# Chunks 2 and 3 of x arrive in columns from DRAM and are normalised there, in place of transposes on TensorE

## The chip, the cores and the metric

The kernel runs on one core of one Trainium2 chip. A time is the device time of one execution in microseconds (us); where several runs are given, it is their median. The profiled execution is a run of its own, recorded with every instruction of every engine: TensorE (PE, and PEld for its weight loads), VectorE (DVE), ScalarE (ACT), GpSimd (POOL) and SyncE (SP). Transfers between DRAM and SBUF are issued on SP and POOL.

## The reference

x has 2048 tokens of 448 features in fp32, the hidden width F is 1792. Cut to what matters:

```python
m = mean(x, axis=-1); v = var(x, axis=-1)
xn = (x - m) / sqrt(v + 1e-5)                       # layernorm, no scale or shift

a = xn @ dft_hid_re.T;  b = xn @ dft_hid_im.T       # DFT along the features
s = dft_seq_re @ a - dft_seq_im @ b                 # real part of the DFT along the tokens

g = silu((gelu(xn @ w_gate) * (xn @ w_up)) @ w_down)
out = x + s * g
```

Every product needs the normalised x. The gate and up products contract over the features, so they want x transposed: features on the partitions, tokens in the columns. The mean and the variance of a token run over the features, that is over a row of x as it lies in DRAM.

## The kernel before, in words

**Split operands.** Every fp32 operand of a product is kept as a high part (an ACT copy into the type `fp32r`, or a DVE copy) and a low part (DVE: source minus high part). A product is three matmuls: high x high, high x low, low x high.

**Chunks.** The 2048 tokens are 4 chunks c = 0..3 of 512. A row of 448 features is padded to 512, so a chunk is four tiles k = 0..3 of 128 tokens by 512 (a partition holds one token), in `xr[c]`. `xr[0]`, `xr[1]` share one buffer (`u0`), `xr[2]`, `xr[3]` another (`u1`). Transposed, a chunk is `xth[c]` and `xtl[c]`, its high and low parts, each with four blocks of 128 features by 512 tokens.

**Layernorm of a chunk (`stats`, L134).** It runs on two or four tiles at a time: `one(i)` makes `bn_stats` and `bn_aggr` on DVE (mean and variance of each token, L140, L141); `root()` takes the square root on ACT (L145) and prepares a factor on DVE; `newton()` is four tiny DVE operations that refine the reciprocal root (L149 to L153); `norm(i)` subtracts the mean and multiplies by the reciprocal root over one 128x512 tile (L158).

**Transposes.** `turn_mm(c, k)` (L164) issues four TensorE transposes of 128x128 of the normalised tile `k` into one of two PSUM banks (kind "tp", banks 4 and 5). `turn_split` (L170) copies the result to `xth` on ACT (L172); for chunks 0 and 1 it makes one more ACT copy of two of the four blocks into `xf` (L175), which the Strassen sums use later; and it subtracts on DVE for `xtl` (L178). After the last tile of a chunk, `whole(c)` (L186) rebuilds the full value in DRAM, in `xw[c]`: SP stores the high parts, POOL adds the low parts with an accumulating transfer. For chunks 0 and 1 it does that for two blocks (512 KB each way), for 2 and 3 for all four (1024 KB each way). Later stages read single blocks back from `xw` (`t_load`).

**Stages.** Each hidden group of 256 is two blocks f. `load_w`, `prep_w`: gate and up weights of f = 0, 1. `gu_mm` (L325) and `first` (L543): gate and up products of one f and one chunk into two PSUM banks of kind "mm" (banks 0 to 3). `act` (L347): GELU on ACT (L351), times the up product on DVE (`m`, L354), high part on ACT (`h`, L355), low part on DVE (`l`). `gateup(f, c, w, between)` (L359) is both, with other work in between. `down_one` (L370): the six matmuls of one tile of 128 tokens with `w_down` (L376) into a bank of kind "o" (banks 6 and 7; kind "po" later), then an ACT copy into `gacc[c]` for the first group (L385), a DVE addition for the later ones (L387). `down` calls it four times for a chunk. `gacc[0]`, `gacc[1]` share a buffer (`a_g[0]`), `gacc[2]`, `gacc[3]` another (`a_g[1]`).

The blocks f = 0 and 1 are done plainly, for all four chunks; this is the part that the change touches. The blocks f = 2 to 13 use a Strassen-like scheme (`strassen`, L412, matmuls L398 and L410) over pairs of chunks; its operands are sums of blocks of the chunks, made on DVE (`sums0`, with `combine`) or from blocks read back from `xw` (`t_load`, `t_step`, `q_steps`). Its weights come with `load_s` on SP (512 KB each) and are summed by `sums_s` and split by `split_s`. After it come the DFT along the features (L989), that along the tokens (L1173 and on) and the output.

**Order.** All is under `manual_schedule` (L505): each engine executes its instructions in the order in which the program issues them, and the two DMA queues take theirs in the order in which SP and POOL reach them. Nothing reorders them; a queued instruction waits until its inputs are there and its output buffer is free. The main part (L506 to L753) is one list written by hand: loads of chunk 0, warm-up matmuls, chunk 0's layernorm and transposes, its gate and up products by halves of 256 tokens, chunk 1's layernorm and transposes in between, statistics of chunk 2 from L613 on and its transposes around `down(0, 0, ...)`, chunk 3's statistics after them. Then a loop over c = 2, 3 (L712) runs gateup(0, c), down(0, c - 1) with chunk 3's transposes as its in-between work, and gateup(1, c). So `down(0, 1)` follows gateup(0, 2).

## Time and profile before

| what | value |
|---|---|
| time, median of 3 runs (lowest to highest) | 774.39 us (774.26 to 774.78) |
| span of the profiled execution | 770.7 us |
| TensorE busy | 764.0 us, 99% |
| VectorE busy | 638.5 us, 83% |
| ScalarE busy | 347.4 us, 45% |
| GpSimd busy | 124.9 us, 16% |
| chain that ended last | PE 95%, DVE 2%, DMA 1% |
| moved by DMA | 165.46 MB, mean 215 GB/s |

The span is the time from the first to the last recorded instruction of one profiled execution; it is shorter than the time of a run by what lies around it. "Busy" sums the time in which an engine executes something. The chain that ended last goes back from the last instruction, at each step to what released it, or to the instruction before it on its engine. In groups of instructions a row has: line, engine, operation, output<-inputs with partitions x elements and type, count | busy us, mean ns of one | idle time of the engine just before them, and what ended most of it. In a DMA row: output<-input, queue, kind, count, KB of each, median us from issue to landing. In lists of single instructions the first number is the start in the span, the second the duration, both in us; "x4" means that four of a kind are taken together. In a table by windows each engine has busy us and the count of instructions in that stretch.

### The profile page before, as it was taken

The numbers are of one execution on the slowest core, as the hardware profiler recorded it, in microseconds if no ns is written. First come the engines' busy times: TensorE is split into PE (matmuls) and PEld (weight loads), VectorE is DVE, ScalarE is ACT, GpSimd is POOL, SyncE is SP. The second block draws the span as 40 slices with busy tenths as digits, with TensorE's granted clock in tenths as the row PEclk, the third lists the DMA queues.
The fourth block names the chain that finished last, engine by engine and source line by source line (L and its number), as shares of the span: only waits on it lengthen the run. The fifth ranks groups of instructions, "written<-read, shape, count | busy, mean of one in ns | idle before, by whom it ended". The sixth has DMA issues, their size and how long they took to land.

```text
span 770.7 us, 11500 instructions
## 1 busy us (share of the span) xinstructions
PE 764.0 (99%) x4052; PEld 688.3 (89%) x4052; DVE 638.5 (83%) x1093; ACT 347.4 (45%) x490; POOL 124.9 (16%) x162
## 2 busy tenths in 40 slices
PE   9999999999999999999999999999999999999997
PEld 8988888888888888888889999999999999999996
DVE  7978989898988988887885676889788796969797
ACT  3756444452533444344334855544444444444441
POOL 2003242332423323323200000000000000000000
PEclk9999999999999999999999999999999999999999
DMA  8479666566767746465652641879797969697894
GB/s 316 91 201 284 153 223 180 148 238 186 252 130 265 199 164 154 154 150 191 138 187 95 268 191 53 255 255 276 262 307 223 343 204 348 189 341 211 311 286 166
DMA packets 81322, 165.46 MB, mean 215 GB/s; under 512 B 8048, under 2 KB 62704, under 8 KB 79728
## 3 DMA queue, kind: packets, MB, share of 16 engines
q1 hardware_dynamic: 75648, 137.15, 51.7%
q0 software_dynamic: 5472, 27.46, 16.7%
q8 instruction: 32, 0.52, 0.3%
q14 instruction: 26, 0.21, 0.1%
q10 hardware_dynamic: 144, 0.11, 0.0%
HBM read 140.71 MB, written 53.35 MB: 252 GB/s over the span
## 4 chain that ended last, share of the span: by engine, by line
PE 95%; DVE 2%; DMA 1%; issue 0%; ACT 0%; SPq 0%; DVEq 0%
PE x L398 24%; PE p L1173 21%; PE po L376 18%; PE p L1176 10%; PE ab L989 9%; PE x L410 4%; PE gu L325 3%; PE py L1193 1%; PE py L1195 1%; PE py L1194 1%; DMA raw<-wgu 1%; PE gu L543 1%; PE pt L167 1%; DVE st L140 0%; DVE xr L158 0%
## 5 line engine op out<-in xcount | busy, mean ns | idle before, releaser
L376 PE MATMUL po<-wd,hs 128*128 128x448 f32 x672 | 152.7, 366 | 0.0
L376 PEld LDWEIGHTS po<-wd,hs 128*128 128x128 f32 x672 | 125.8, 188 | 14.2
L398 PE MATMUL x<-xt,w 128*128 128x512 f32 x450 | 119.4, 391 | 0.0
L398 PEld LDWEIGHTS x<-xt,w 128*128 128x128 f32 x450 | 84.4, 188 | 16.4 <-DVE tmp L444 0.4
L127 ACT ACTIVATE w<-raw 128x896 fp32r<-128x896 f32 (+1 forms) x59 | 53.7, 912 | 63.1 <-DVE raw L1079 35.4
L398 PE MATMUL x<-t,w 128*128 128x512 f32 x276 | 79.7, 391 | 0.0
L387 DVE TENSOR_TENSOR gacc<-gacc,po 128x448 f32<-128x448 f32 x96 | 58.5, 615 | 12.4 <-PE po L376 12.3
L989 PE MATMUL ab<-w,xt 128*128 128x448 f32 x256 | 68.1, 365 | 0.0
L398 PEld LDWEIGHTS x<-t,w 128*128 128x128 f32 x276 | 51.8, 188 | 9.3
L1218 POOL DMA_DIRECT2D cc<-x x14 | 12.4, 882 | 289.3 <-DVE raw L1078 107.8
L475 ACT ACTIVATE hs<-tmp 128x512 fp32r<-128x512 f32 x24 | 15.2, 634 | 97.4 <-DVE tmp L473 97.4
L1173 PE MATMUL p<-xt,w 128*128 128x448 f32 x168 | 54.3, 374 | 0.0
L276 POOL TENSOR_TENSOR raw<-raw 128x256 f32<-128x256 f32 x23 | 18.5, 806 | 211.9 <-DMA raw<-wss 177.4
L989 PEld LDWEIGHTS ab<-w,xt 128*128 128x128 f32 x256 | 48.1, 188 | 3.8
L127 ACT ACTIVATE w<-f 128x896 fp32r<-128x896 f32 (+1 forms) x34 | 30.2, 889 | 42.1 <-DVE f L1079 21.1
L128 DVE TENSOR_TENSOR w<-raw,w 128x896 fp32r<-128x896 f32 (+1 forms) x40 | 41.8, 1046 | 3.3 <-ACT w L127 2.7
L1078 DVE TENSOR_TENSOR raw<-raw 128x128 f32<-128x128 f32 x69 | 19.8, 287 | 21.2 <-DMA raw<-sums 21.1
L293 ACT ACTIVATE w<-raw 128x768 fp32r<-128x768 f32 x24 | 20.3, 846 | 36.7 <-POOL raw L280 36.7
L1173 PE MATMUL p<-ts_u,ts_tmp 128*128 128x448 f32 x112 | 36.3, 374 | 0.0
L1173 PE MATMUL p<-ts_g,w 128*128 128x448 f32 x112 | 36.3, 374 | 0.0
L410 PE MATMUL x<-xt,w 128*128 128x512 f32 x116 | 35.9, 390 | 0.0
L1173 PE MATMUL p<-hs,w 128*128 128x448 f32 x112 | 35.6, 374 | 0.0
(267 smaller groups left out, 1842.8 us busy)
## 6 DMA issues: line engine op xcount, KB each, us to landing
sums<-ca SPq DMA_DIRECT2D x16, 896.0 KB, 8.7
sums<-ca POOLq DMA_DIRECT2D x16, 896.0 KB, 8.6
raw<-ct SPq DMA_DIRECT2D x69, 192.0 KB, 4.4
raw<-wss SPq DMA_DIRECT2D x24, 512.0 KB, 3.9
ts_u<-td SPq DMA_DIRECT2D x24, 448.0 KB, 6.3
ts_g<-td SPq DMA_DIRECT2D x24, 448.0 KB, 6.5
raw<-sums SPq DMA_DIRECT2D x69, 128.0 KB, 4.4
f<-ct SPq DMA_DIRECT2D x39, 192.0 KB, 3.8
```

Source lines behind the costliest of these rows:

```text
L127: nc.scalar.activation(h, src, AF.Copy)
L128: nc.vector.tensor_sub(l, src, h)
L293: nc.scalar.activation(h[:, :n], src[:, :n], AF.Copy)
L325: nc.tensor.matmul(ps[:, cols], a, xt[:, k, cols], start=n == 0, stop=n == len(mm) - 1)
L376: nc.tensor.matmul(po[:, :D], hs[:, a, kk * P : (kk + 1) * P], wdn[:, b, i], start=n == 0, stop=n == 5,)
L387: nc.vector.tensor_add(ga, ga, po[:, :D])
L398: nc.tensor.matmul(ps, a[i], b[j], start=first and n == 0, stop=n == 2, skip_group_check=True)
L410: nc.tensor.matmul(ps, a[0], x_, start=False, stop=True, skip_group_check=True)
L989: nc.tensor.matmul(p[:, :D], a, b, start=n == 0, stop=n == len(mm) - 1)
L1078: nc.vector.tensor_add(s2, cr1, s1)
L1173: nc.tensor.matmul(ps[q][:, :D], h, v, start=u % UN == 0, stop=False, skip_group_check=True)
L1176: nc.tensor.matmul(ps[q][:, :HD], l, v[:, :HD], start=False, stop=u % UN == NS - 1, skip_group_check=True,)
```

## The change

Chunks 2 and 3 get a second input: `xt`, the same values of x in columns, 128 features by (4 blocks x 512 tokens), 1 MB for each chunk, with the four tiles' tokens interleaved (column 4q + k of a block is token q of tile k). The host's array is x itself, permuted. What remains to be done in columns is to subtract a mean and multiply by a reciprocal root that differ from column to column and are the same in every partition.

- `load_xt(2)` brings chunk 2's columns on SP into the buffer of `gacc[2]`, `gacc[3]`, behind the loads of the first weights; `load_xt(3)` brings chunk 3's into `xr[3]`, once its statistics are taken from it.
- Chunk 2's statistics are taken on ACT: four passes `mean2` (negated mean by the sum of a row, `accum_out`) and four passes `square2` (sum of squares around the mean), `root2` on ACT, `newton2` (five operations) on DVE. Chunk 3's stay on DVE (`bn_stats`), in a new order.
- `spread(c)` writes the reciprocal roots and negated means of the 512 tokens to DRAM (`vec[c]`, 4 KB), reads the roots back to all 128 partitions (`tmp(c - 2)`, 256 KB), and adds the negated means to the columns by two accumulating transfers on POOL, each of 512 KB, whose source is one row of 2 KB read by every partition.
- `scale(c, i)` multiplies half a chunk (128x1024) by the roots on DVE; it reads its inputs with a step of four elements and writes the tokens in plain order. `scaled_high` (ACT copy of 128x1024) and `scaled_low` (DVE subtraction of 128x1024) make the two parts. The scaled columns are stored to `xw[c]` by one 1024 KB transfer of SP.
- The transposes of chunks 2 and 3, their `turn_split`, their `norm` and their two accumulating stores are gone.
- `down(0, 1)` now stands ahead of gateup(0, 2), `down(0, 2)` after gateup(0, 3) as before; `down(0, 0)` and `down(0, 1)` take banks 4 to 7 in turn (kind "d") in place of 6 and 7. The loop over c = 2, 3 is written out; `sums_s`, `load_s`, `load_d` and `sums0` have new places in the list.

```diff
-    turns = {"mm": 1, "tp": 0, "o": 0, "x": 0, "po": 0, "all": 0}
+    turns = {"mm": 1, "tp": 0, "o": 0, "x": 0, "po": 0, "all": 0, "d": 3}
...
-        first, n = {"mm": (0, 4), "tp": (4, 2), "o": (6, 2), "x": (0, 5), "po": (5, 3), "all": (0, 8)}[kind]
+        first, n = {"mm": (0, 4), "tp": (4, 2), "d": (4, 4), "o": (6, 2), "x": (0, 5), "po": (5, 3), "all": (0, 8)}[kind]
...
     def whole(c):
-        n = 1024 if c < 2 else 0
-        h, l = [a_x[c][:, 2048 * i + n : 2048 * (i + 1)].bitcast(F32) for i in range(2)]
-        nc.sync.dma_start(xw[c][:, n:], h)
-        nc.gpsimd.dma_start(xw[c][:, n:], l, accum_op=ALU.add)
+        h, l = [a_x[c][:, 2048 * i + 1024 : 2048 * (i + 1)].bitcast(F32) for i in range(2)]
+        nc.sync.dma_start(xw[c][:, 1024:], h)
+        nc.gpsimd.dma_start(xw[c][:, 1024:], l, accum_op=ALU.add)
+    vec = {c: dram.tile([2, 512], F32, name=f"vec{c}") for c in (2, 3)}
+    vt = {c: const.tile([P, 2, 4], F32, name=f"vt{c}") for c in (2, 3)}
+    columns = {2: a_g[1][:, :2048], 3: xr[3].rearrange("p a b -> p (a b)")}
+    scaled = {2: xr[2].rearrange("p a b -> p (a b)"), 3: a_g[1][:, :2048]}
+
+    def load_xt(c):
+        nc.sync.dma_start(columns[c], xt[c - 2])
+
+    def spread(c):
+
+        nc.sync.dma_start(vec[c].rearrange("a (p k) -> p a k", k=4), vt[c])
+        nc.sync.dma_start(tmp(c - 2), vec[c][0].partition_broadcast(P))
+        for i in range(2):
+            nc.gpsimd.dma_start(
+                part(columns[c], 1024 * i, 2, 512),
+                vec[c][1].partition_broadcast(P).unsqueeze(1).to_broadcast([P, 2, 512]),
+                accum_op=ALU.add,
+            )
+
+    def scale(c, i):
+
+        n = slice(1024 * i, 1024 * (i + 1))
+        src = columns[c][:, n].rearrange("p (b q k) -> p b k q", b=2, k=4)
+        dst = scaled[c][:, n].rearrange("p (b k q) -> p b k q", b=2, k=4)
+        r = tmp(c - 2).rearrange("p (q k) -> p k q", k=4)
+        nc.vector.tensor_mul(dst, src, r.unsqueeze(1).to_broadcast([P, 2, 4, P]))
+        if i:
+            nc.sync.dma_start(xw[c], scaled[c])
+
+    def scaled_high(c, i):
+        n = slice(1024 * i, 1024 * (i + 1))
+        nc.scalar.activation(a_x[c][:, n], scaled[c][:, n], AF.Copy)
+
+    def scaled_low(c, i):
+        n = slice(1024 * i, 1024 * (i + 1))
+        nc.vector.tensor_sub(a_x[c][:, 2048:][:, n], scaled[c][:, n], a_x[c][:, n])
...
+        po = in_turn("po" if sends[0] else "d", f"po{gi}_{c}_{kk}")
...
         draw = load_d(GROUPS[0])
+        load_xt(2)
         first(0, half[0], ("hh", "hl", "lh", "last"))
...
+        def mean2(k):
+            nc.scalar.activation(
+                tmp(1)[:, :D], xr[2][:, k, :D], AF.Identity, scale=-1.0 / D,
+                accum_out=vt[2][:, 1, k : k + 1],
+            )
+
+        def square2(k):
+            nc.scalar.activation(
+                tmp(1)[:, :D], xr[2][:, k, :D], AF.Square, bias=vt[2][:, 1, k : k + 1],
+                accum_out=w2[:, 0, k : k + 1],
+            )
+
+        def root2():
+            nc.scalar.activation(w2[:, 1], w2[:, 0], AF.Sqrt, bias=epst, scale=1.0 / D)
+
+        def newton_to(r, t, w):
+            nc.vector.reciprocal(r, t)
+            nc.vector.tensor_mul(t, r, r)
+            nc.vector.tensor_mul(t, t, w)
+            nc.vector.scalar_tensor_tensor(r, t, 1.5, r, op0=ALU.add, op1=ALU.mult)
+
+        def newton2():
+            nc.vector.tensor_scalar(w2[:, 0], w2[:, 0], -0.5 / D, -0.5 * EPS, op0=ALU.mult, op1=ALU.add)
+            newton_to(vt[2][:, 0], w2[:, 1], w2[:, 0])
+
+        mean2(0)
+        mean2(1)
         root()
+        mean2(2)
+        mean2(3)
         newton()
         norm(0)
         norm(1)
         one, root, newton, norm = stats(1, 2, 2)
         one(0)
         one(1)
+        for k in range(4):
+            square2(k)
         root()
+        root2()
         first(0, half[1], ("hh", "lh"))
...
         newton()
         norm(0)
         norm(1)
+        newton2()
+        spread(2)
         turn_split(t0, t1)
-        one, root, newton, norm = stats(2, 0, 4)
...
         one(2)
         one(3)
-        root()
+        load_xt(3)
+        nc.scalar.activation(sd[:, 1], mv[:, :, 1], AF.Sqrt, bias=epst)
+        nc.vector.tensor_scalar(sd[:, 0], mv[:, :, 1], EPS, -0.5, op0=ALU.add, op1=ALU.mult)
+        nc.vector.tensor_scalar(vt[3][:, 1], mv[:, :, 0], -1.0, None, op0=ALU.mult)
         l0()
-        newton()
-        norm(0)
-        norm(1)
+        newton_to(vt[3][:, 0], sd[:, 1], sd[:, 0])
+        spread(3)
         l1()
         first(0, half[1], ("hh", "lh", "hl", "last"), 1, pg)
-        norm(2)
-        norm(3)
         m0, h0, l0 = act(0, 1, pg)
         m0()
         pg = gu_ps(1, 1)
         for g in range(2):
             gu_mm(pg[g], ws[1], g, 1, slice(0, 512))
-        turn_split(turn_mm(2, 0))
         h0()
-        between = [lambda k=k: turn_split(turn_mm(2, k)) for k in (1, 2, 3)]
-        turn = between[0]
-        between[0] = lambda: (turn(), l0())
-        down(0, 0, wdn, between)
+        scale(2, 0)
+        l0()
         m1, h1, l1 = act(1, 1, pg)
-        one, root, newton, norm = stats(3, 0, 4)
-        one(0)
-        one(1)
+        scaled_high(2, 0)
         m1()
         h1()
-        one(2)
-        one(3)
-        root()
-        l1()
-        newton()
-        norm(0)
-        norm(1)
+        scale(2, 1)
+        down(0, 0, wdn, [l1, lambda: scaled_high(2, 1), lambda: scaled_low(2, 0), lambda: scaled_low(2, 1)])
+        draw = load_d(GROUPS[1])
+        load_s(2)
+        down(0, 1, wdn)
         t0 = {}
...
-        for c in (2, 3):
...
-            down(0, c - 1, wdn, between)
...
+        scale(3, 0)
+        scaled_high(3, 0)
+        scale(3, 1)
+        scaled_high(3, 1)
+        scaled_low(3, 0)
+        scaled_low(3, 1)
+        sums_s(nc.vector)
+        m0, h0, l0 = gateup(0, 2, ws[0])
+        m0()
+        h0()
+        l0()
+        sums0()
+        m1, h1, l1 = gateup(1, 2, ws[1])
+        m1()
+        t_load(0, 0, 3, 2)
+        h1()
+        l1()
+        for v in split_s(slots[0]):
+            v()
+        w_of[0, 2] = parts_of(slots[0])
+        load_s(3)
+        m0, h0, l0 = gateup(0, 3, ws[0])
+        m0()
+        h0()
+        l0()
+        down(0, 2, wdn, [lambda: t_split0(1), lambda: t_split0(2)])
+        nwdn, low_d = prep_d(GROUPS[1], draw)
+        m1, h1, l1 = gateup(1, 3, ws[1], [lambda: t_split0(3), lambda: (t_split0(4), q_steps[0][0]())])
+        m1()
         late = (h1, l1)
```

59 lines of the change are left out of this document (16 added, 43 removed).

## The prediction, made before the changed kernel ran

> **What bounds the kernel now.** I read the first part of the page for the whole, then what TensorE waited for, then the chain of waits over the first 140 us, where the change lies. In the groups the columns are busy time, mean ns of one, and idle time before; in the chain they are start, duration, what.
>
> ```profile
> span 770.7 us, 11500 instructions
> PE 764.0 (99%) x4052; PEld 688.3 (89%) x4052; DVE 638.5 (83%) x1093; ACT 347.4 (45%) x490; POOL 124.9 (16%) x162
> PE warm L524 <- DVE hs L514: 1.5, 1, 1.5
> PE gu L543 <- ACT xt L172: 0.3, 1, 0.3
> 20.85 0.19 DVE mv L141
> ...
> 21.07 0.30 ACT sd L145
> 21.37 0.98 ACT xt L172 x2
> ...
> 22.39 1.69 PE gu L543 x12
> 24.08 1.03 PE pt L167 x8
> 25.11 3.84 PE gu L543 x32
> 28.95 5.02 PE gu L325 x22
> 33.97 0.44 PE pt L167 x4
> ...
> 54.34 0.44 PE pt L167 x4
> ...
> 67.18 5.02 PE gu L325 x22
> 72.19 4.08 PE x L398 x18
> ```
>
> TensorE is busy 99%, and its recorded waits are the start-up and 0.3 us at 22.4 us. From 22.39 us on the chain runs through TensorE without a gap, through the first Strassen product at 72.19 us and beyond. So there are two regimes. Before 22.4 us the chain hops between DVE and ACT: a delay there moves everything. After it only TensorE work, or a new wait of TensorE, counts.
>
> **Removed: eight groups of transposes.** Chunks 2 and 3 lose 32 transposes, eight groups of four. The chain has them one by one, the first at 33.97 and the last at 54.34 us, each 0.44 us: 8 x 0.44 = 3.52 us off TensorE's path. Their 8 ACT copies and 8 DVE subtractions, the 8 normalisations and two accumulating 1024 KB transfers into `xw` go too; all lay beside TensorE work, so they are worth nothing directly, but they make room for what is added.
>
> **Added in the head: chunk 2's statistics on ACT, its Newton steps on DVE.** Eight passes over 128x448 (four `mean2`, four `square2`) and a second root enter ACT between 16.0 and 21.1 us; five tiny DVE operations (`newton2`) enter DVE between chunk 1's normalisation and its first `turn_split`.
>
> ```profile
> 7.25 1.28 SPq L132 DMA_DIRECT2D xr<-x  x3
> 2.03 0.20 ACT L518 ACTIVATE tbl<-epst 128x1 f32<-128x1 f32 x1
> 15.37 0.67 ACT L175 ACTIVATE tmp<-pt 128x256 f32<-128x256 f32 x2
> 16.62 0.30 ACT L145 ACTIVATE sd<-mv,epst 128x2 f32<-128x2 f32 x1 [0.59 <-DVE mv L141]
> 22.20 1.00 DVE L158 TENSOR_SCALAR xr<-xr,mv,sd 128x512 f32<-128x512 f32 x2
> 23.12 1.28 DVE L178 TENSOR_TENSOR xt<-pt,xt 128x512 fp32r<-128x512 f32 x2
> 24.45 0.42 PEld L167 LDWEIGHTS pt<-ident,xr 128*128 128x128 f32 x4 [0.17 <-DVE xt L178]
> xr<-x SPq DMA_DIRECT2D x3, 1024.0 KB, 8.2
> L385 ACT ACTIVATE gacc<-po 128x448 f32<-128x448 f32 x12 | 6.5, 543 | 6.2 <-PE po L376 6.2
> L172 ACT ACTIVATE xt<-pt 128x512 fp32r<-128x512 f32 x14 | 8.1, 594 | 5.9 <-PE pt L167 5.9
> L355 ACT ACTIVATE hs<-tmp 128x512 fp32r<-128x512 f32 x8 | 5.0, 633 | 5.1 <-DVE tmp L354 5.1
> L152 DVE TENSOR_TENSOR sd<-sd 128x4 f32<-128x4 f32 x2 | 0.3, 168 | 0.1
> ```
>
> Chunk 2 is the middle one of the three loads issued from 7.25 us, so it is issued near 7.7 and, at the middle landing time of 8.2 us, there by 15.9: no wait for it. A pass reads SBUF: the copy of 128x448 took 0.543, and a copy of 128x512 from SBUF 0.633 where one from PSUM took 0.594, so about 0.58. Each waits for the one before (about 0.03), so 0.61 for a mean. The squares also take their bias from a tile: the root of 128x2 with its bias took 0.30 and the 128x1 one without that second operand 0.20, so 0.71. No row shows what the added sum per row costs. The low end is nothing, the high end one more smallest instruction of 0.30 us each. A copy with 448 elements is the nearest row in every respect but that output, so I take nothing and keep 8 x 0.30 = 2.4 us for the range.
>
> ACT is free at 15.37 + 0.67 = 16.04. Two means end at 17.26, chunk 1's first root (0.30) at 17.56, still before DVE asks for it at 17.8; two means end at 18.78, four squares at 21.62. The second root, which starts at 21.07 before, starts 0.55 later. DVE is late by that, then runs five operations of 0.17 + 0.03 = 1.0 us, and only then the two subtractions (23.12 us before). The next transposes reuse the banks those free: the idle 0.17 us at 24.45 shows TensorE already waiting there, so the delay passes on whole. Head: 0.55 + 1.0 = +1.55 us; the copies at 21.37 slip 0.85 by the second root and lie inside that. A gain is excluded, nothing is removed before 22 us.
>
> **Chunk 2's columns must arrive in time.** The path is `newton2`, a 4 KB write of statistics, then on POOL two accumulating transfers of 512 KB that add the negated mean, read from one 2 KB row by every partition, then `scale`. `scale(2,0)` stands on DVE between the product of gate(0,1) and what that chunk still needs; `scaled_high(2,0)` stands on ACT ahead of h1 and of the eight PSUM drains L385 of the moved down products. If the transfer is late, DVE and ACT stop with all that queued, and TensorE stops at chunk 1's first down product, for which bank 4 and h1, l1 are needed.
>
> ```profile
> 33.18 0.60 ACT L351 ACTIVATE tmp<-gu 128x512 f32<-128x512 f32 x1
> xw<-xt POOLq DMA_DIRECT2D x2, 512.0 KB, 5.8
> xw<-xt POOLq DMA_DIRECT2D x2, 1024.0 KB, 8.0
> cc<-x POOLq DMA_DIRECT2D x14, 224.0 KB, 6.8
> sp<-xt SPq DMA_DIRECT2D x4, 512.0 KB, 10.4
> xr<-x SPq DMA_DIRECT2D x2, 256.0 KB, 2.8
> out<-cc SPq DMA_DIRECT2D x1, 112.0 KB, 1.7
> ```
>
> Need: the GELU of (0,1) at 33.18 ends 33.78; later by 1.55 and one more small DVE operation (0.20) it ends at 35.5, the product at 36.2, where `scale(2,0)` can start; `scale(2,1)` follows a scale, l0 and m1, at 38.5. Supply: `newton2` ends at 23.2 + 0.55 + 1.0 = 24.75; the small write lands 1.7 to 2.8 later, at 26.5 to 27.5; an accumulation of 512 KB took 5.8 (into SBUF, for 224 KB, 6.8), so the first half is there at 32.3 to 34.3; the two halves together are 1024 KB, 8.0, so the second at 34.5 to 35.5. Spare time: 1.9 us or more on the first, 3.0 on the second. I cost it at nothing. TensorE has some 0.7 us in hand (its chunk 0 down products end near 40.3, l1 near 40.9 is wanted a bit later), so a second half later than 38.5 by x costs x - 0.7. The column load itself (1 MB behind the weights on SP at about 9 us) has until 27 us. On POOL the accumulation for `xw1` now stands behind those of chunk 2; its reader comes after 46 us. SP holds `load_d` and `load_s(2)` behind `scale(2,1)`, near 39.7, as they are held until 40.5 us before.
>
> Chunk 3 has its Newton steps at 34.4, its statistics in DRAM by 37.5, so columns by 37.5 + 8.0 = 45.5; TensorE needs them near 55, after 24 + 24 down products (9.7 us) and two gate/up products of 5.02 us each. DVE in between has two scales, two lows, the sums of `load_s(2)`, four sums of chunk 0 and 1 and the products of chunk 2 queued, some 12 us: done by 57.5, wanted at 60. The store of `xw3` leaves at 46.6 the buffer that the down products of chunk 2 fill from 60 us; even at 8.0 us it is gone. Nothing. That `down(0,1)` moves ahead of gateup(0,2) exchanges TensorE work of the same length, and its four banks replace two: nothing either.
>
> **The scales.** Each is a product of 128x1024 whose two inputs are read with a step of 16 bytes; no row shows such a step.
>
> ```profile
> L297 DVE TENSOR_TENSOR w<-raw,w 128x768 fp32r<-128x768 f32 x1 | 1.0, 951 | 0.0
> L315 DVE TENSOR_TENSOR wd<-raw,wd 128x896 fp32r<-128x896 f32 x1 | 1.1, 1074 | 0.0
> L209 DVE TENSOR_TENSOR tmp<-tmp 128x512 f32<-128x512 f32 x1 | 0.7, 684 | 0.0
> L689 DVE TENSOR_TENSOR tmp<-tmp 128x512 f32<-128x512 f32 x1 | 1.2, 1222 | 0.0
> ```
>
> From 768 to 896 elements is 0.123 us, so 1024 take 1.20: the low end. The high end is the slowest that DVE ran such an operation, 1.222 against 0.684 for 512, 1.79 times, so 2.14. Plain rows of this shape are nearest, I take 1.20: then `l1` of (1,1) ends near 40.4 and TensorE does not wait. At 2.14 the two scales ahead of l1 bring it 1.9 us later, of which TensorE has about 0.9 in hand: +1.0 us.
> [...]
>
> **The sum.** -3.52 + 1.55 = -1.97 us. The profiled span of 770.7 us stands 3.7 below the median of 774.39 of the three runs; what lies around the span I take as fixed. 774.39 - 1.97 = 772.4 us. What a measurement of this kernel can tell from no change is about 0.2%, 1.55 us: faster is below 772.8, slower above 775.9.
>
> **Rivals.**
> - *The new instructions are dear.* Row sums at up to 0.30 each (+2.4), strided scales (+1.0). For it: neither output nor step is in any row. Against it: at the low ends it vanishes. With a 0.20 read-out the time is 772.4 + 1.6 = 774.0, with the scales 775.0, with both high ends 775.8: within 0.2%. Chance 0.29.
> - *The spread is late* (the other side). 128 partitions read one 2 KB row, and the transfers accumulate into SBUF. If the halves go one after the other at 6.8 us the second lands at 41 and costs 1.8 us, 774.2; at the 10.4 us that 512 KB took when the queues were full, 27.5 + 20.8 = 48.3, 9.1 us, 781.5. It eats the whole gain when the second half lands later than 38.5 + 0.7 + 1.97 = 41.2, and is slower by over 0.2% from 42.7. For it: no row repeats a source, and the DMA engines are 0.72 and 0.70 busy from 25 to 35 us already (last column but one below). Against it: 3 us to spare, and part of that load (the accumulation for `xw1`) now comes after. A middle case is 777. Chance 0.31, of which 0.27 beyond the bound.
>  [...]
> - *The statistics hide.* If ACT's passes finish before 21.07, only `newton2` is left: 774.39 - 3.52 + 1.0 = 771.9. Chance 0.04.
>
> ```profile
> 25.00:30.00 5.00, 5.00 (x40) 4.78 (x39) 4.82 (x9) 4.71 (x9) 0.09 (x1) 1.00 0.72 193
> 30.00:35.00 5.00, 5.00 (x26) 4.24 (x25) 4.72 (x15) 4.23 (x6) 0.79 (x1) 1.00 0.70 103
> ```
>
> **How the numbers follow.** The forecast has 0.36; its own range is 771.4 to 772.8. With the statistics hidden (0.04) it makes faster 0.40. Dear instructions give 0.24 and a spread late by little 0.04 to same, 0.28. The spread beyond the bound, 0.27, and both high ends with some lateness on top, 0.05, make slower 0.32. The range goes from 771.2 to 779.5 and leaves out a badly late spread.
>
> **What the changed profile would show.** The chain without transposes between 30 and 60 us and the first Strassen product near 70.2 us. TensorE idle near 22 to 26 us some 1.5 us longer; far more would mean that the row sums cost. Scale operations of 1.2 us; 2.1 would mean the step costs. No wait of DVE for a transfer into `gacc` or `xr`; a wait there, with TensorE idle at a down product near 40 us, would make the prediction wrong by just that wait.

## The result: 793.5 us, 2.6% slower

| | before | after |
|---|---|---|
| time, median of the runs taken side by side (4 and 4) | 774.33 us (772.99 to 774.78) | 793.53 us (793.07 to 794.11) |
| span of the profiled execution | 770.7 us | 792.2 us |

The ratio is 1.0256, with a 95% interval of 1.0241 to 1.027. The forecast was 772.4 us with a range up to 779.5, so the kernel is 19 us slower where a gain of 2 was forecast.

The first rows are the head of the page of the kernel after; behind the dots stand the larger waits of TensorE over the whole execution (us in total, times, longest).

```profile
span 792.2 us, 11454 instructions
PE 768.1 (97%) x4020; PEld 683.8 (86%) x4020; DVE 640.3 (81%) x1078; ACT 349.4 (44%) x500; POOL 129.8 (16%) x164
...
PE po L410 <- DVE hs L390: 4.8, 1, 4.8
PE po L410 <- ACT gacc L419: 2.4, 1, 2.4
PE po L410 <- ACT hs L389: 2.0, 1, 2.0
...
PE x L432 <- ACT tmp L490: 1.5, 2, 1.0
PE x L432 <- DVE tmp L483: 1.3, 4, 0.5
PE x L432 <- DVE tmp L511: 1.2, 1, 1.2
PE x L432 <- DVE tmp L522: 1.0, 1, 1.0
```

Before, TensorE had one wait of 0.3 us after its start. After, it waits 9.2 us at three down products (`po`) and some 6 us in the Strassen stage (`x`), a stage that the change does not touch. So there are two losses, and they come at different times. The first Strassen product starts at 82.65 us where it started at 72.03 before: 10.6 us late. The last matmul of the kernel starts 21.9 us late. Half of the loss lies ahead of the first Strassen product and half behind it.

**The early loss.** Next come single instructions of the kernel after, taken from its lists by engine and brought together by subject: the two transfers that add chunk 2's means and the two for chunk 3 (POOL), the four scales (DVE), and what TensorE does at the gate and up product of 30 us, at its waits and at the first Strassen product. The brackets give the idle time in front of an instruction and what ended it.

```profile
28.47 1.23 POOL L202 DMA_DIRECT2D gacc<-vec  x1 [2.26 <-DMA vec<-vt]
38.69 1.22 POOL L202 DMA_DIRECT2D gacc<-vec  x1 [8.99 <-issue]
46.57 1.23 POOL L202 DMA_DIRECT2D xr<-vec  x1 [5.72 <-issue]
54.30 1.21 POOL L202 DMA_DIRECT2D xr<-vec  x1 [6.50 <-issue]
...
38.46 2.01 DVE L214 TENSOR_TENSOR xr<-gacc,tmp 128x1024 f32<-128x1024 f32 x1 [2.31 <-DMA gacc<-vec]
46.27 1.97 DVE L214 TENSOR_TENSOR xr<-gacc,tmp 128x1024 f32<-128x1024 f32 x1 [4.61 <-DMA gacc<-vec]
54.01 2.02 DVE L214 TENSOR_TENSOR gacc<-xr,tmp 128x1024 f32<-128x1024 f32 x1 [2.89 <-DMA xr<-vec]
60.94 1.97 DVE L214 TENSOR_TENSOR gacc<-xr,tmp 128x1024 f32<-128x1024 f32 x1 [4.92 <-DMA xr<-vec]
...
30.36 5.18 PE L359 MATMUL gu<-xt,w 128*128 128x512 f32 x22
42.81 1.29 PE L410 MATMUL po<-wd,hs 128*128 128x448 f32 x5 [2.41 <-ACT gacc L419]
48.90 5.58 PE L410 MATMUL po<-wd,hs 128*128 128x448 f32 x19 [4.79 <-DVE hs L390]
82.65 0.84 PE L432 MATMUL x<-xt,w 128*128 128x512 f32 x3
```

Against them stand these rows of the kernel before: the same gate and up product, one group of the transposes that are gone and the product behind it, and the first Strassen product.

```profile
28.78 5.18 PE L325 MATMUL gu<-xt,w 128*128 128x512 f32 x22
33.80 0.60 PE L167 MATMUL pt<-ident,xr 128*128 128x128 f32 x4
34.16 1.47 PE L376 MATMUL po<-wd,hs 128*128 128x448 f32 x6
72.03 0.84 PE L398 MATMUL x<-xt,w 128*128 128x512 f32 x3
```

Every scale waits for its transfer. Chunk 2's halves are there at 38.4 and 46.2 us, where the forecast had 34.3 and 35.5 at the latest, and chunk 3's second half at 60.9 instead of 45.5. The second transfer of a pair is issued only when the first has landed: POOL stands idle for 9 us in front of it, and no instruction of the program is named as the reason ("issue"). Behind the waiting scale stand the low parts of chunk 1 on DVE and the drains of the down products on ACT, and TensorE stops for both, as the prediction had said of a late transfer.

The stops cost a second time. These are the busy times of the engines and TensorE's granted clock (column behind POOL) in three stretches of the kernel after:

```profile
40.00:45.00 5.00, 1.70 (x7) 0.88 (x6) 1.67 (x3) 2.55 (x4) 0.85 (x1) 1.00 0.81 101
45.00:50.00 5.00, 1.10 (x3) 1.01 (x4) 3.73 (x4) 1.72 (x3) 1.23 (x1) 0.53 1.06 192
50.00:55.00 5.00, 5.00 (x21) 4.47 (x20) 2.11 (x2) 2.21 (x5) 0.70 (x1) 0.79 1.02 314
```

TensorE's clock is at one half from 45.3 to 52.1 us, 6.8 us long; the first stop lies at 40.40 to 42.81 us, the second at 44.11 to 48.90. In 48.9 to 52.1 it works at that clock, and a matmul starts each 0.37 us there and each 0.20 behind it, which costs 1.6 us. The account up to the first Strassen product reads: +1.6 that the head is late (28.78 to 30.36), -2.9 for the transposes (a group takes 0.36 us from its start to the start of the next product, 33.80 to 34.16), +9.2 of waits, +1.6 of clock, together +9.5 of the 10.6 us. The remaining 1.1 us are about what the matmuls at the edges of the stops lose: by their starts, the one ahead of a stop takes some 0.16 us more than others, the one behind it 0.10.

**The late loss.** In the Strassen stage each block loads its weights (`raw<-wss`) on SP, and POOL sums them. In the fence are SP's issues and POOL's work near 134 us, in the kernel after. Behind the second dots stands the row of the DMA queue that fetches instructions, counted between 133.5 and 135.5 us alone (packets, MB, share of the 16 DMA engines).

```profile
133.52 0.33 SPq L294 DMA_DIRECT2D raw<-wss  x1
133.96 1.88 SPq L295 DMA_DIRECT2D raw<-wss  x1
...
140.02 0.74 POOL L310 TENSOR_TENSOR raw<-raw 128x256 f32<-128x256 f32 x1 [10.94 <-DVE tmp L470]
144.54 1.65 POOL L840 DMA_DIRECT2D sums<-ca  x2
147.30 0.33 SPq L294 DMA_DIRECT2D raw<-wss  x1
...
q8 instruction: 1, 0.02, 4.6%
```

The same load in the kernel before, POOL's accumulating transfers behind it, and the next load:

```profile
120.28 0.39 SPq L261 DMA_DIRECT2D raw<-wss  x1
128.06 1.68 POOL L775 DMA_DIRECT2D sums<-ca  x2
133.62 0.33 SPq L260 DMA_DIRECT2D raw<-wss  x1
```

The second issue takes 1.88 us, where the same issue of the kernel before takes 0.39, and a 16 KB transfer of that instruction queue runs at the same moment. The load lands at 139.86 (5.9 us after its issue; before 3.7), and POOL's sums begin 0.16 us behind that; the row names a DVE instruction as what ended the wait, and I take the load for it, which the row of the restored kernel below names. The accumulating transfers `sums<-ca`, which stand on POOL behind the sums, are issued at 144.54. They come 2.8 us ahead of the next load of weights, where before it was 5.6. That load then takes 10.0 us (before 7.2), and TensorE waits for what hangs on it. Two more fetches fall on loads of weights in this stage: the issue `raw<-wd` at 222.56 us takes 2.27 us, where others take 0.38, and that at 252.32 us takes 0.38 beside a fetch at 252.26. From 75 to 330 us no fetch falls on an issue of SP in the kernel before. The experiments below test whether the fetch is the cause.

### The profile page after: what moved, and what is told of

Read it like the earlier page. It is cut to its first block, busy times and chain, and to the rows that moved or that the text cites. A ratio compares the mean times of both kernels' runs of the same rounds, so it can differ in the third digit from the quotient of the medians.

```text
span 792.2 us, 11454 instructions
## 1 busy us (share of the span) xinstructions
PE 768.1 (97%) x4020; PEld 683.8 (86%) x4020; DVE 640.3 (81%) x1078; ACT 349.4 (44%) x500; POOL 129.8 (16%) x164
## 4 chain that ended last, share of the span: by engine, by line
PE 66%; DVE 13%; DMA 11%; ACT 4%; issue 3%; POOL 1%; SPq 0%; DVEq 0%; POOLq 0%; ACTq 0%
PE p L1238 18%; PE x L432 13%; PE po L410 10%; PE ab L1054 9%; PE p L1241 9%; DMA raw<-wss 3%; PE x L444 3%; DMA tmp<-xw 2%; DMA ts_g<-td 2%; PE py L1258 1%; PE py L1260 1%; PE py L1259 1%; DMA tmp<-vec 1%; DMA vec<-vt 1%; DVE w L324 1%
## 6 DMA issues: line engine op xcount, KB each, us to landing
sums<-ca POOLq DMA_DIRECT2D x16, 896.0 KB, 10.2
```

## The experiments

A time "at the first Strassen product" is the start of TensorE's first `x` matmul after the start of the span. It stands against 72.03 us in the kernel before. "Late at the end" is the time by which the last matmul is late.

### Without the mean subtraction

The kernel after without its four accumulating transfers: columns, statistics, roots, scales and order stay. Its output lacks the subtraction of the mean in chunks 2 and 3.

```diff
-        for i in range(2):
-            nc.gpsimd.dma_start(part(columns[c], 1024 * i, 2, 512),
-                vec[c][1].partition_broadcast(P)..., accum_op=ALU.add)
```

> The changed kernel without the two pairs of accumulating transfers that add the negated means: the columns are scaled as they came, so the output lacks the means; everything else, the statistics included, stays. Theory A (the late second accumulation is the cause): scale(2,0) finds its input ready at 36.2 us, the chain has no DMA into gacc or xr, TensorE has no gap over 1.5 us between 35 and 55 us, and of the 21.8 us that TensorE ends later only the head (+1.4 us at 30 us) and about 1.2 us for the dear scales remain against the 3.52 us of transposes: 774.4 - 3.5 + 1.4 + 1.2 = 773.5 us, 772 to 776. Rival B (the order of the work, DVE's scales and lows ahead of the sums and the products, is too much whatever DMA does): over 783 us. Rival C (half and half, other transfers of the change are late too): 776 to 783 us.

Measured: 778.4 us, ratio 1.0063 (1.0046 to 1.0081), above theory A's 776 and in the range of rival C. Rival C's reason is not what the trace shows: TensorE has no recorded wait from 28 to 75 us, and the first scale starts at 36.34 us, where the prediction needed it at 36.2. The first Strassen product starts at 70.94 us, 1.1 earlier than before. So the four transfers make all of the early loss: with them 10.6 us late, without them 1.1 us early. Of the 2.0 us that the sum promised for the early stage, 1.1 are there once the transfers are gone: in this execution the head costs 1.8 us, and the missing transposes gain 2.9. Yet the run is slower than the kernel before: from -1.1 it goes to +5.6 us at 257 us and to +6.6 at the end. The late loss is there without a late transfer.

A second run leaves out, beside the means, the interleaved order of the columns, so that the scales read and write plain rows.

> As the run without the means, and the scales read and write their 128x1024 elements in plain order, so that the tokens come out permuted: the same count of elements with no step of 16 bytes. Theory A: the scales take 1.2 us in place of 1.99 us, and TensorE's small waits at chunk 1's down products go: 772.3 us, about 1.2 us under the run without the means. Rival: the step costs more than that, because the four scales stand ahead of later work on DVE: 4 x 0.8 = 3.2 us under it. If the scales still take 2 us, the cost is not the step but the broadcast operand.

Measured: 778.2 us, ratio 1.0051 (1.0034 to 1.0068). The row has two scales of this run; with the step they took 1.97 to 2.02 us, as shown above:

```profile
L207 DVE TENSOR_TENSOR xr<-gacc,tmp 128x1024 f32<-128x1024 f32 x2 | 2.4, 1219 | 0.0
```

A step of 16 bytes costs 0.8 us per scale: 2.0 against 1.22. The forecast's choice of 1.20 fits the plain rows and was wrong for the step. The time shows no effect of it, against the theory (1.2 us) and the rival (3.2 us): the two runs differ by 0.2 us. This was tested only where the means are not added and the scales have room.

### The head alone

The kernel before with the statistics of chunk 2 on ACT, the second root and `newton2`, which are computed and stored and not used.

> The kernel before, with the eight passes of statistics on ACT, the second root, the five operations on DVE and the small write of 4 KB added at the places that the change gives them; the results are not used, chunks 2 and 3 keep their transposes and their own statistics. Theory A: the head alone costs what the changed trace shows at 30 us, +1.4 us, and it goes through to the end: 775.8 us (775.2 to 776.5). Rival: work that follows has slack for it, 774.4 us, within 0.4. Rival: more than the shift, because DVE is later for all that follows by the same amount: over 777 us.

Measured: 774.95 us, ratio 1.002 (1.0003 to 1.0038); the first Strassen product comes 0.98 us late and the end 0.92. TensorE's matmuls ahead of the head are 0.5 us early in this execution, so the head costs 1.5 us, what the forecast made it. (The +1.4 of the expectations sets the chain's 28.95 us against 30.36; from start to start it is 1.58.) The lateness stays between 0.9 and 1.2 us from there to the end: a delay of 1 us alone brings no late loss.

### Why the columns are late: the row, the queue, or the accumulation

The first kernel writes the row of means twice, so that a partition's 4 KB come as one piece instead of two of 2 KB.

```diff
...
-                part(columns[c], 1024 * i, 2, 512),
-                vec[c][1].partition_broadcast(P).unsqueeze(1).to_broadcast([P, 2, 512]),
+                columns[c][:, 1024 * i : 1024 * (i + 1)],
+                vec[c][1:].rearrange("a d -> (a d)").partition_broadcast(P),
```

> The negated means stand twice in DRAM, so that each accumulating transfer of 512 KB has 128 rows of 4 KB in place of 256 rows of 2 KB; one 2 KB write more on SP, nothing else changed. In the changed kernel the second transfer of a pair was issued 10.2 us after the first, 0.25 us after the first had landed, though POOL was free and no wait of the program stands before it; the accumulation for xw1, of 128 rows, was issued 0.7 us after that second one without waiting. Theory A1 (the queue of POOL holds a limited number of rows, over 384 and under 512): the second is now issued within 2 us of the first, both have landed near 40 us in place of 46.3, and the time falls to about 780 us (774 to 787). Rival (an accumulation into SBUF waits for the one before, whatever its rows): the second still waits for the first, 793 us, within 1.5.

The second lets each partition read its own 4 KB of `xt` instead of the one row.

```diff
-                vec[c][1].partition_broadcast(P).unsqueeze(1).to_broadcast([P, 2, 512]),
+                xt[c - 2][:, 1024 * i : 1024 * (i + 1)].rearrange("p (a d) -> p a d", a=2),
```

> The changed kernel, but the four accumulating transfers read 128 distinct rows of the column array in place of the one row of means for all partitions (so what is added is not the negated mean). Sizes, descriptors and targets are the same. Theory (accumulating 1 MB into SBUF takes about 14 us whatever it reads): the second half of chunk 2 still lands 16 to 19 us after the first was issued, time 790 to 796. Rival (the one row, read 128 times over, is the limit): both halves land within 10 us of the first issue, at 35 to 39 us, DVE does not wait for them, and the time falls to 780 to 786.

Measured: 792.99 us, ratio 1.0244 (1.0227 to 1.0262), for the wide rows; 787.66 us in one run for the own rows. POOL's issues and the second scale of chunk 3 in each, wide rows ahead of the dots:

```profile
29.04 1.78 POOL L203 DMA_DIRECT2D gacc<-vec  x2 [1.60 <-DMA vec<-vt]
60.74 1.96 DVE L215 TENSOR_TENSOR gacc<-xr,tmp 128x1024 f32<-128x1024 f32 x1 [1.31 <-DMA xr<-vec]
```

```profile
25.14 2.15 POOL L202 DMA_DIRECT2D gacc<-xt  x2
56.61 1.96 DVE L214 TENSOR_TENSOR gacc<-xr,tmp 128x1024 f32<-128x1024 f32 x1 [1.85 <-DMA xr<-xt]
```

In pieces of 4 KB both transfers of a pair are issued together ("x2"). So POOL's 9 us of "issue" hang on how a transfer is cut: with 256 pieces of 2 KB the second was issued 10.2 us behind the first (28.47 and 38.69), with 128 of 4 KB both took 1.78 us together. That half of the theory held; the landing near 40 us and the time near 780 did not come. The pair still needs 14.5 us from the first issue to the second landing (29.04 to 43.51, where the kernel after had 46.25), and chunk 3's columns are ready at 60.7 as before: the small write of its means now takes 12.0 us, so its pair is issued at 47.03 us only. The own rows came out as 4 KB pieces too (864 packets on POOL's queue from 24 to 62 us in both, 1376 in the kernel after), so they are compared with the wide rows and not with the kernel after, as their expectation had it. They need 14.05 us (25.14 to 39.19), and the time lies between the ranges of the theory and the rival. One row or 128 rows makes a difference of 0.4 us for a pair, in one execution of each. In the kernel after, half a megabyte from one row landed 7.6 us after its issue (38.69 to 46.25).

The own rows are 5 us faster than the wide ones. They don't wait for the statistics: their first pair is issued 3.9 us earlier and chunk 3's, at 42.58 us, 4.5. They show what the early loss hangs on. The second scale of chunk 3 starts at 60.94, 60.74 and 56.61 us in the kernel after, with wide rows, and with own rows; the first Strassen product follows at 82.65, 83.80 and 78.31 us, 21.7 to 23.1 us later each time.

### Without accumulation at all

Here the means go to all partitions with a plain transfer of 256 KB, POOL adds them in place, both chunks' variances come from `bn_stats`, and the gate and up products of chunks 2 and 3 take the high parts first. This and two later kernels hold 32 or 16 matmuls of 16x16 in the warm-up; the section after next tells why.

```diff
+    def shift(c):
+        for i in range(2):
+            v = part(columns[c], 1024 * i, 2, 512)
+            nc.gpsimd.tensor_add(v, v, tmp(0).unsqueeze(1).to_broadcast([P, 2, 512]))
```

> A version without accumulating transfers: both chunks come in columns, the negated means come by a plain 256 KB transfer that spreads one row over the partitions, and POOL adds them in place; the variances come from bn_stats on DVE at their old places; gate/up of chunks 2 and 3 take the high parts first; with the 32 small matmuls. Theory (the accumulating transfers and nothing else in the column scheme made the change dear in the early stage): first Strassen product at 68.5 to 74 us against 72.0 before, time 771 to 776. Rival (the strided scales and the queues of DVE and ACT make it dear, however the means come): DVE late at gate/up of chunk 2 and 3 by 3 us or more each, 778 or more.

Measured: 784.9 us, ratio 1.013 (1.009 to 1.0169), the first Strassen product 9.0 us late. The rival's time came. Its waits came in part: TensorE waits 2.4 us at the gate and up products of chunk 2 and 1.6 at those of chunk 3, under the 3 us each that it named. A further 2.5 us, at a down product, have a reason that neither had named. Single instructions of that kernel on POOL and DVE:

```profile
31.82 4.70 POOL L204 TENSOR_TENSOR gacc<-gacc,tmp 128x1024 f32<-128x1024 f32 x2 [6.38 <-DMA tmp<-vec]
31.98 2.25 DVE L655 TENSOR_TENSOR sd<-vt 128x4 f32<-128x4 f32 x1
34.26 2.28 DVE L656 TENSOR_TENSOR sd<-sd 128x4 f32<-128x4 f32 x1
...
47.42 0.17 DVE L655 TENSOR_TENSOR sd<-vt 128x4 f32<-128x4 f32 x1
```

A DVE operation on 128x4 takes 0.17 us, and 2.25 and 2.28 while POOL adds 128x1024: the second ends at 36.54 us, POOL's additions at 36.52. The low part that the down product waits for stands on DVE behind these two. While POOL makes chunk 3's two additions, three more DVE operations, two of 128x1024 and one of 128x512, take 7.4 us in place of 3.1. So POOL's additions are not free work. How much of the 9.0 us hangs on them was not tested apart.

### Chunk 3 alone in columns

Chunk 2 stays as it was before. Chunk 3's means are taken early on ACT, and its transfers are issued at 25.6 us, 30 us ahead of their use.

> One part alone: only chunk 3 comes in columns, chunk 2 stays as in the kernel before. Chunk 3's means are taken by ACT early and its accumulating transfers are issued near 20 to 27 us, some 30 us ahead of their use; 16 small matmuls stand for its 16 removed transposes. Theory (the scheme itself is sound where the 14 us of the accumulation lie ahead of their use): no wait of TensorE for the scaled columns, four groups of transposes less (-1.8 us), head +0.3 to +0.6 us for the means: 773 to 774.5. Rival (the strided scales and the fuller queues of DVE and ACT in chunk 2's and 3's stage cost more than the transposes): TensorE waits some 3 us at gate/up of chunk 3, 776 to 778.

Measured: 779.13 us, ratio 1.007 (1.0045 to 1.0095), above both ranges. The accumulation is hidden: it lands at 34.8 us, 9.2 us after its issue. Now the roots are late, which come from `bn_stats` at the old place. The second kernel computes and sends them earlier, ahead of the weight loads on SP.

```diff
-        draw = load_d(GROUPS[1])
-        load_s(2)
         spread_root()
...
+        load_s(2)
+        draw = load_d(GROUPS[1])
```

> Only chunk 3 in columns again, with its roots sent earlier: the statistics of chunk 3 stand on DVE between the splits of chunk 2, the spread of the roots leaves SP ahead of the weight loads instead of behind them, and the sums of the weights stand behind the scales on DVE. Theory (the 4.2 us that TensorE waited in the run before hung on the roots, which landed at 55.5 us): the roots land by 50 to 52 us, TensorE waits 1 us or less at gate/up of chunk 3, first Strassen product at 70.5 to 72.5 us, time 772 to 775. Rival (the scales and the lows, some 8 us of DVE and ACT, are the limit): still 2 us or more of waits, 776 to 779.

Measured: 779.87 us, ratio 1.0064 (1.0047 to 1.0081), above both ranges again. TensorE's waits for the scaled columns fall from 4.2 to 3.0 us and the first Strassen product from 76.75 to 74.42 us. The roots of 256 KB are still late. The first row is chunk 3's scales in the first kernel, the second one in the second:

```profile
55.58 3.86 DVE L222 TENSOR_TENSOR xr<-gacc,tmp 128x1024 f32<-128x1024 f32 x2 [4.78 <-DMA tmp<-vec]
```

```profile
53.90 3.88 DVE L222 TENSOR_TENSOR xr<-gacc,tmp 128x1024 f32<-128x1024 f32 x2 [5.27 <-DMA tmp<-vec]
```

DVE is idle for 5 us in front of the scales in both. The theory (roots by 50 to 52 us) failed: the transfer was issued 3.7 us earlier, at 45.75, and took 8.1 us instead of 6.0, with an accumulation for `xw` and the weight loads beside it. Neither kernel with chunk 3 alone beat the kernel before; chunk 2 alone was not tried.

### The late loss: instruction fetches

The pieces of 16 KB on the queue q8 "instruction" come 32 times in the kernel before (0.52 MB) and 31 times in the kernel after (0.51 MB). I read them as TensorE's instructions, by their number: 4052 matmuls with as many weight loads make 253 for each piece, and the 4020 of the kernel after 259. From the first piece to the last (17.57 to 760.97 us before, 20.04 to 769.50 after) TensorE starts 7876 matmuls and weight loads in 31 intervals before and 7601 in 30 after, 254 and 253 for an interval; the expectations below put it at 256. The change takes 32 transposes, 64 instructions with their weight loads, out of the front of that stream, so each later piece is asked for at another point of the work: at 116.6 us before, between two loads of weights; at 134.0 us after, on a load. To test this, 32 matmuls of 16x16 that compute nothing needed stand in place of four of the warm-up matmuls. They bring the count back.

```diff
-        warm(WARM)
+        warm(WARM - 4)
+        t = o_tile("tiny")
+        for _ in range(32):
+            nc.tensor.matmul(t[:16, :16], junk[:, :16], junk[:, :16], start=True, stop=True)
```

Once in the kernel without means, once in the whole changed kernel:

> The kernel without the mean subtraction (778.4 us), with 32 matmuls of 16x16 put in place of four of the fourteen warm-up matmuls at the start, so that TensorE's stream has again as many instructions ahead of the Strassen products as before the change. Theory (the late loss comes from the fetch of TensorE's instructions, 16 KB every 256 instructions, which falls on the load raw<-wss of the three-block products): the fetch falls at 116 to 118 us again as in the kernel before, the load ahead of 133 us takes about 7.2 us instead of 9 to 10.5, and the stretch from the first Strassen product to the end is as long as in the kernel before within 1 us: 772.5 to 774.0. Rival (the late loss comes from the order in which the queues reach the Strassen stage, whatever is fetched): 778.4 again, within 1 us, with the same waits of TensorE for DVE's tmp at about 135, 178 and 220 us.

> The changed kernel whole, with the same 32 matmuls of 16x16 in place of four warm-up matmuls. Theory of the fetch: the early loss stays (about +10.6 us at the first Strassen product), of the later 11.2 us some 6 go: 786 to 789. Rival (the later loss is a matter of the order of the queues): 793.5 within 1.5.

And the other way round: the kernel before with nothing of the change, its stream shifted by 192 instructions.

```diff
-        warm(WARM)
+        t = o_tile("tiny")
+        for _ in range(96):
+            nc.tensor.matmul(t[:16, :16], junk[:, :16], junk[:, :16], start=True, stop=True)
+        for _ in range(WARM):
+            nc.tensor.matmul(t[:, :288], junk[:, :P], junk[:, :288], start=True, stop=True)
```

> The kernel before with nothing of the change, but with 96 matmuls of 16x16 added to the warm-up, whose 14 matmuls are cut from 512 to 288 columns so that it takes about as long. TensorE's stream is so shifted by 192 instructions, as far against a raster of 256 as the 64 that the change takes away shift it the other way. Theory (the place of the instruction fetches alone makes the late loss): the fetch that fell at 116.6 us falls near 120 or 133 us, one of the loads raw<-wss there takes over 4.5 us, and the stretch from the first Strassen product to the end is 3 to 6 us longer: 777 to 780. Rival (the late loss belongs to the change itself): 774 to 775.5.

In the table, the lateness at 100, 130 and 257 us is that of one matmul, counted from the first Strassen product on, against its time in the kernel before.

| kernel | time | ratio (95%) | late at the first Strassen product | at 100 us | at 130 us | at 257 us | late at the end |
|---|---|---|---|---|---|---|---|
| after | 793.53 | 1.0256 (1.0241 to 1.027) | +10.6 | +13.9 | +13.7 | +20.7 | +21.9 |
| after, count restored | 787.29 | 1.0159 (1.0127 to 1.019) | +11.6 | +14.2 | +13.9 | +14.6 | +14.8 |
| without means | 778.4 | 1.0063 (1.0046 to 1.0081) | -1.1 | +1.0 | +0.8 | +5.6 | +6.6 |
| without means, count restored | 775.22 | 1.0002 (0.9987 to 1.0018) | -0.3 | +1.1 | +0.9 | +1.5 | +3.8 |
| before, count shifted | 782.21 | 1.01 (1.0077 to 1.0124) | +0.5 | +4.5 | +4.6 | +9.1 | +10.2 |

The columns of lateness compare one execution of each kernel with one of the kernel before, whose span of 770.7 us is short: the runs of the kernel before beside these experiments have spans with medians from 772 to 773 us. By the medians of the times the five kernels are 19.2, 12.5, 4.6, 0.4 and 7.2 us slower, 2 to 3.4 less than the last column.

Shifting the stream alone makes the kernel before 1% slower, more than the theory's 777 to 780, with 9.7 of its 10.2 us behind the first Strassen product. Restoring the count takes 8.1 us of the late loss out of the changed kernel (11.3 to 3.2), within the theory's range, and 3.5 out of the one without means (7.6 to 4.1), whose time lies 1.2 us above the theory's range. What it takes out stands between 130 and 257 us: the changed kernel loses 7.0 us there, and 0.7 with the count restored. SP's issues and POOL's at the same load show the path, first in the changed kernel with the count restored, then in the shifted kernel before:

```profile
134.16 0.38 SPq L295 DMA_DIRECT2D raw<-wss  x1
137.95 0.74 POOL L310 TENSOR_TENSOR raw<-raw 128x256 f32<-128x256 f32 x1 [9.74 <-DMA raw<-wss]
141.87 1.65 POOL L843 DMA_DIRECT2D sums<-ca  x2
```

```profile
124.91 1.27 SPq L261 DMA_DIRECT2D raw<-wss  x1
134.17 1.66 POOL L779 DMA_DIRECT2D sums<-ca  x2
```

With the count restored the issue is back at 0.38 us, POOL starts at 137.95 instead of 140.02, and the accumulation leaves 2.7 us earlier. Where the fetch falls on it, the issue takes 1.27 us. From that issue to the accumulation it is 7.8 us in the kernel before, 10.6 in the changed one, 7.7 with the count restored and 9.3 in the shifted one. That the place of the fetch sets most of the late loss is shown from both sides. The step within, that the fetch itself holds up SP's issue, is read from the coincidence in these rows and was not tested apart.

Not all of the late loss goes this way. Between the first Strassen product and 100 us, in the table's terms, DVE waits for one load `tmp<-xw` of 256 KB, on whose issue no fetch falls. It lands 5.0 us after its issue in the kernel before, 10.5 in the changed kernel, 9.5 with the count restored and 13.0 in the shifted kernel. So 2.6 of the 3.2 us that remain with the count restored stand there, and 4.0 of the shifted kernel's 9.7. What makes that load late is open. In the restored kernel without means 2.3 of the remaining 4.1 us come behind 600 us, and their cause is open too. The restored kernels have four warm-up matmuls fewer and reach the first Strassen product 0.8 and 1.0 us later than the same kernels without the small matmuls; the one without means starts its first gate and up product at 10.65 us, the kernel before at 9.09.

### Filling the stops

The clock's fall was tested in the changed kernel: 28 matmuls that compute nothing needed stand where TensorE waits, 10 ahead of the first stop and 18 ahead of the second.

```diff
+                if (gi, c, kk, n) == (0, 1, 0, 5):
+                    fill(18, wdn)
...
+        fill(10, wdn)
         down(0, 1, wdn)
```

> The changed kernel with 28 matmuls of 128x448 that compute nothing needed (their bank is not read), put on TensorE where it waits for the late columns: 10 ahead of chunk 1's first down product of that group, 18 ahead of that product's last matmul. They also restore TensorE's instruction count, so the run stands beside the one with the small matmuls at the start (787.3 us, granted clock 0.5 from 45.1 for 10.2 us). Theory (TensorE's idle time of 2 us and more is what halves the granted clock): with the waits filled the clock stays 1.0 between 40 and 60 us, and the time falls by half of what TensorE worked at half clock, some 3 us: 783 to 785.5. Rival (the clock falls for another reason, such as the rush of transfers or the work before it): half clock for 7 to 10 us as before, 786.5 to 789.

The same stretch as above, in this kernel:

```profile
40.00:45.00 5.00, 4.07 (x20) 3.46 (x19) 1.97 (x3) 2.56 (x4) 1.15 (x2) 1.00 0.78 103
45.00:50.00 5.00, 4.34 (x22) 3.70 (x21) 3.94 (x4) 1.91 (x4) 1.23 (x1) 1.00 1.05 197
50.00:55.00 5.00, 5.00 (x25) 4.39 (x25) 1.72 (x2) 2.07 (x5) 0.51 (x1) 1.00 1.02 323
```

The clock stays at 1.00 from 40 to 55 us, so the stops did cause its fall. The time is 786.19 us, ratio 1.0156 (1.013 to 1.0182), against 787.29 with the count restored and no filling; the intervals overlap, and the gain of 3 us did not come. Chunk 3's columns are ready at 60.87 us as before, and TensorE, which is earlier, waits for their consequences later: 1.7 us ahead of gate/up of chunk 3 and 2.0 at the next down product. The half clock was a consequence that cost little, because the stage ends with the columns. This kernel also bears on the late loss: its warm-up is that of the changed kernel, its count is made up at 40 to 48 us, and its lateness only goes from 12.1 us at the first Strassen product to 13.6 at the end.

## Why the prediction was wrong

- **The spread was costed at nothing, and this step failed.** The need was right: without the means the first scale starts at 36.34 us, for 36.2 forecast. The supply was wrong. Its rows (512 KB in 5.8 us, 1024 KB in 8.0) came from accumulations into DRAM, and the one row into SBUF, 224 KB in 6.8 us, was taken for 512 KB as it stood. Here chunk 2's pair took 17.8 us in the kernel after (28.47 to 46.25), 14.5 in pieces that are issued together, and 9.2 in the run with chunk 3 alone, where all queues together move 197 GB/s in that time, for 262 in the 14.5 us. What the estimate lacked: the accumulation of chunk 0's `xw`, issued 3.3 us ahead on the same queue; the column load and the stores that run beside it; and a queue that took the second transfer only when the first had landed (issued at 38.69 us, the first half there at 38.4). The last is shown by the wide rows, where both were issued within 1.78 us; what each of the others weighs was not tested apart. The spare 1.9 and 3.0 us became waits of 2.3 and 4.6 us of DVE. For chunk 3 the estimate of 45.5 us missed by 15 us: its first half is issued at 46.57 us, just behind the landing of chunk 2's second half at 46.25, and its second half only when the first has landed. Its small write took 7.4 us where 3.1 were forecast, but was done by 41.7.
- **The rival "the spread is late" had the mechanism and the place right** (DVE held at the scale, l1 and the drains behind it, TensorE at the down product). For chunk 2 its price fits too: by its rule, a second half at 46.25 us costs 46.25 - 38.5 - 0.7 = 7.0 us, and TensorE waits 7.2 at those two stops. But it said nothing of chunk 3, which sets the end of the stage, and nothing of the stage behind. One of its reasons, that the halves go one after the other, is what happened; the other, one row for all partitions, is refuted by the own rows. The range left a badly late spread out, by its own words.
- **The sign of being wrong came**, a wait of DVE for a transfer with TensorE idle at a down product, at 40.4 us. That the error would be just that wait did not hold: 9.2 us of waits stand against a time 21 us above the forecast.
- **The transposes** were forecast at -3.52 us and are worth 2.9. The 0.44 us of the chain's rows count a part of each group that overlaps with the product behind it; from start to start a group takes 0.36. The kernel without means gains as much: 1.8 us late ahead of the first group, 1.1 early at the first Strassen product.
- **The head** was forecast at +1.55; it measured +1.58 at 30 us and 1.5 alone, so it was right. A mean takes 0.58 us and a read of the sum 0.19, at a pitch of 0.70 together; a square 0.67 and 0.19, at 0.79. So a row sum costs 0.1 us net and not the 0.30 of the high end.

```profile
17.45 0.56 ACT L636 ACTIVATE tmp<-xr 128x448 f32<-128x448 f32 x1
17.92 0.19 ACT L636 ACTIVATION_READ_ACCUMULATOR tmp<-xr 128x1 f32 x1
19.64 0.67 ACT L642 ACTIVATE tmp<-xr,vt 128x448 f32<-128x448 f32 x1
```

- **The scales** took 2.0 us, near the high end of 2.14 and not the 1.20 chosen. The run in plain order, without the means, shows no effect of this on the time.
- **The late loss** of 11 us (by the medians some 9) stands in no step and no rival. The sum took for granted that, once the Strassen products begin, the rest of the kernel is only moved in time. Taking instructions out of TensorE's stream changed when their fetches come, and most of this loss is that (8.1 of 11.3 us go when the count is restored); some 3 us of it stand at one late load, whose reason is open.

## What to carry to other kernels

A transfer that the compute waits for is priced from the row of its own queue at that time, with what is already queued and running beside it, and for every user of it, not only the first; here the last one set the time. Look for early issue: for the same accumulation, issued 30 us ahead of its use, no engine waited. And when instructions are added or removed and a far later stage changes its speed, compare where the instruction fetches fall before looking for a reason in that stage; putting the count back with empty instructions is a cheap test.

## What the hardware showed that was not expected

- A fetch of 16 KB, read as TensorE's instructions (the one at 134 us in the kernel after took 4.6% of 16 DMA engines' time over 2 us, 1.5 us of one engine), coincides with issues on SP that take 1.27 (shifted kernel before), 1.88 and 2.27 us (kernel after) instead of 0.38; one issue beside a fetch, at 252.32 us in the kernel after, took 0.38. Shifting the fetches' place alone made the kernel before 1% slower (782.21 us).
- POOL's queue took two accumulating transfers of 128 pieces each at once (1.78 us for both, wide rows), and of 256 pieces only one after the other (28.47 and 38.69 us, kernel after); one of 256 and one of 128 stood in it together (issued at 38.69 and 39.42 us there).
- Behind a stop of TensorE of 2.0 us (filled kernel, up to 72.80 us) 21 matmuls took 6.45 us together; behind one as long in the kernel after (up to 72.87 us) the same 21 took 4.91, with a granted clock of 1.00 from 70 to 75 us. With two stops close together the granted clock was at one half for 6.8 us (2.4 and 4.8 us, kernel after) or 10.2 us (4.2 and 3.5, count restored).
- A DVE operation of 0.17 us took 2.25 us beside a POOL addition of 128x1024 (kernel without accumulation, 31.98 us).
